# Gate and up of a SwiGLU kernel as two 128x64 weight halves side by side in the array

## The chip, the cores and the metric

The kernel runs on one core of a Trainium2 chip. The metric is the device time of one execution in microseconds; the time before is the median of three runs.

## The reference

```python
B, S, D, F = 1, 2048, 640, 1536          # all bfloat16
def reference(x, w_gate, w_up, w_down):
    g = jax.nn.silu(x @ w_gate)          # [S, D] @ [D, F]
    u = x @ w_up
    return (g * u) @ w_down              # [S, F] @ [F, D]
```

## The kernel before

The 2048 rows of x are worked through in four row blocks of 512 (`NSB`, `S_BLK`). All weights are kept in SBUF, with the contraction dimension D in five steps of 128 partitions (`KD`), and F in twelve chunks of 128 (`KF`). x is kept transposed in `xT`, so that a matmul takes a 128x128 piece of weights as its stationary operand and streams 512 columns of `xT`.

In a row block, for each chunk `fc` of F, `proj` (L202) makes five matmuls into a PSUM tile `pg` with the gate weights, then five into `pu` with the up weights; all ten are recorded at L204. Both tiles are of the tag "gu", which has four buffers of one bank each, so two chunks can be under way. `gate` (L217) lets ScalarE (ACT) take silu of `pg` into `sg` (L221) and VectorE (DVE) multiply `sg` with `pu` into the bf16 tile `aT` (L222). When the twelve chunks are done, the down product follows: twelve matmuls into `po_t` (L287) for the last 128 columns of the output, held transposed, and then for each of the four groups of 128 rows twelve matmuls into `po_a` (L316) for the first 512 columns. ScalarE copies these results out, and DMAs write them.

Row block 0 has a beginning of its own: `head` (L226) warms TensorE up with 20 matmuls (`pw`, L182), turns the first 256 rows of x by ten TensorE transposes (`pt`, L195), and does its first four chunks in pieces as the weights arrive (L250 and, through `proj`, L204). The last row block streams 508 rows instead of 512: the last four rows of x (`T`) get their gate and up on VectorE, by 96 multiply-and-sum instructions (`row_dots`, L153) that `do_dots` spreads out: two behind each of the first ten chunks of row blocks 1 to 3, and three at several places of the down products. The last 128 rows of the output are done in three column pieces of 256, 256 and 128.

The order of TensorE, ScalarE and GpSimd is fixed for the head by `keep_order` (L100), and that of VectorE and of the DMA queue of SyncE for the whole kernel; after the head TensorE's work follows the program in its own order: all gate and up chunks of a row block, po_t, po_a, and then the next row block. TensorE has a load of weights ahead of every matmul.

Of the kernel before, what the change touches and what calls it, by code (L numbers as in the profile page):

```python
# [10 lines left out]
def _body(  # L11
# [8 lines left out]
    nc = tc.nc  # L20
    P = nc.NUM_PARTITIONS
# [11 lines left out]
    KD = D // P  # L33
    KF = F // P
    S_BLK = 512
# [24 lines left out]
    xT = consts.tile([P, KD, S], bf16)  # L60
    wg_sb = consts.tile([P, KD, F], bf16)
    wu_sb = consts.tile([P, KD, F], bf16)
# [47 lines left out]
    def turn_x(c0, c1, k0=0, k1=KD):  # L110
        s_sl = slice(c0 * P, c1 * P)
        nc.sync.dma_start_transpose(out=xT[:, k0:k1, s_sl], in_=xt_v[s_sl, k0:k1])
# [22 lines left out]
    def turn_w(dst, src):  # L135
        for a in range(0, KF, WT_STEP):
            nc.sync.dma_start_transpose(
                out=dst[:, a : a + WT_STEP, :], in_=src[:, a : a + WT_STEP, :]
            )
# [24 lines left out]
    def row_tail():  # L164
        for _ in dots:
            pass
        nc.scalar.activation(row_s[:], row_g[:], ACT.Silu)
        nc.vector.tensor_tensor(
            out=aT[:, :, S - T : S], in0=row_s[:], in1=row_u[:], op=ALU.mult
        )  # L170
# [3 lines left out]
    def do_dots(n):  # L174
        for _ in range(n):
            next(dots, None)
# [25 lines left out]
    def proj(ps, w_sb, fc, sb, c0, c1, k0=0, k1=KD):  # L202
        for kd in range(k0, k1):
            nc.tensor.matmul(  # L204
                ps[:, c0:c1],
                lhsT=w_sb[:, kd, fc * P : (fc + 1) * P],
                rhs=xT[:, kd, sb * S_BLK + c0 : sb * S_BLK + c1],
                start=(kd == 0),
                stop=(kd == KD - 1),
            )  # L210

    def gu_tiles():
        pg = psum.tile([P, S_BLK], f32, tag="gu", name="pg", bufs=4)
        pu = psum.tile([P, S_BLK], f32, tag="gu", name="pu", bufs=4)
        return pg, pu

    def gate(pg, pu, sb, fc, n_s):  # L217

        s0 = sb * S_BLK
        sg = work.tile([P, S_BLK], f32, name="sg")  # L220
        nc.scalar.activation(sg[:, 0:n_s], pg[:, 0:n_s], ACT.Silu)  # L221
        nc.vector.tensor_tensor(  # L222
            out=aT[:, fc, s0 : s0 + n_s], in0=sg[:, 0:n_s], in1=pu[:, 0:n_s], op=ALU.mult
        )
# [46 lines left out]
    for sb in range(NSB):  # L271
        n_s = S_BLK if sb < NSB - 1 else S_BLK - T
        for fc in range(KF):
            if sb == 0 and fc < N_FIRST:
                continue
            pg, pu = gu_tiles()
            proj(pg, wg_sb, fc, sb, 0, n_s)
            proj(pu, wu_sb, fc, sb, 0, n_s)
            gate(pg, pu, sb, fc, n_s)
            if sb > 0 and fc < KF - 2:  # L280
                do_dots(2)


        n_t = (SUB if sb < NSB - 1 else SUB - 1) * P
        po_t = psum.tile([P, n_t], f32, tag="po_b", name="po_t")
        for kf in range(KF):
            nc.tensor.matmul(  # L287
                po_t[:],
                lhsT=wd_sb[:, kf, DA:D],
                rhs=aT[:, kf, sb * S_BLK : sb * S_BLK + n_t],  # L290
                start=(kf == 0),
                stop=(kf == KF - 1),
            )
        ot_t = outp.tile([P, n_t], bf16, name="ot_t")
        ot_q = outp.tile([P, n_t], bf16, name="ot_q")
        nc.scalar.copy(ot_t[:], po_t[:])  # L296
        do_dots(3)
        nc.vector.transpose(out=ot_q[:], in_=ot_t[:])  # L298
        for q in range(P // Q):
            nc.scalar.dma_start(  # L300
                out=out2[
                    sb * S_BLK : sb * S_BLK + n_t, DA + q * Q : DA + (q + 1) * Q
                ].rearrange("(i r) c -> r i c", r=Q),
                in_=ot_q[q * Q : (q + 1) * Q, :].rearrange("r (i c) -> r i c", c=Q),
            )

        for j in range(SUB):
            s0 = sb * S_BLK + j * P
            last = sb == NSB - 1 and j == SUB - 1
            cols = [(0, DA, "po_a")]  # L310
            if last:
                cols = [(0, DA // 2, "po_a"), (DA // 2, DA, "po_a"), (DA, D, "po_b")]
            for c0, c1, tag in cols:
                po = psum.tile([P, c1 - c0], f32, tag=tag, name="po_a")
                for kf in range(KF):
                    nc.tensor.matmul(  # L316
                        po[:],
                        lhsT=aT[:, kf, s0 : s0 + P],
                        rhs=wd_sb[:, kf, c0:c1],
                        start=(kf == 0),  # L320
                        stop=(kf == KF - 1),
                    )
                ot = outp.tile([P, c1 - c0], bf16, name="ot" if c1 < D else "ot_b")
                if c1 < D:
                    nc.scalar.copy(ot[:], po[:])  # L325
                    eng = nc.sync
                else:
                    nc.vector.tensor_copy(out=ot[:], in_=po[:])  # L328
                    eng = nc.sync
                if 0 < j and not last:  # L330
                    do_dots(3)
                if sb == NSB - 1 and j == ROW_J:
                    row_tail()
                eng.dma_start(out=out2[s0 : s0 + P, c0:c1], in_=ot[:])
        if sb == 0:
            turn_x(2 * SUB, 3 * SUB)
            turn_w(wuT, wut_v)
            turn_x(3 * SUB, 4 * SUB)
# [72 lines left out]
def kernel(tc, *args):  # L411
    _body(tc, *args)
    tc.close()
    tc.compile()
    _trim(tc.nc)
# [30 lines left out]
```

## Time and profile before

| | |
|---|---|
| median of 3 runs | 163.79 us (163.2, 163.79, 163.9) |
| profiled execution, its own time | 163.25 us |
| its span, first to last instruction | 161.9 us |
| TensorE matmuls (PE) busy | 159.6 us, 99% of the span, 818 instructions |
| TensorE weight loads (PEld) busy | 79.9 us, 49%, 818 instructions |
| VectorE (DVE) busy | 110.5 us, 68% |
| ScalarE (ACT) busy | 42.6 us, 26% |
| granted TensorE clock | 1.00 |

PE counts the time in which at least one matmul is under way; neighbouring matmuls overlap, so the sum of their durations is more than the busy time, and the distance of their starts is read from the chain of work that ended last, which strings together the groups in order of time. PEld counts weight loads, which can lie beside matmuls.

### The profile page before, as it was taken

The numbers are of one execution on the slowest core, as the hardware profiler recorded it, in microseconds if no ns is written. First come the engines' busy times: TensorE is split into PE (matmuls) and PEld (weight loads), VectorE is DVE, ScalarE is ACT, GpSimd is POOL, SyncE is SP. The second block draws the span as 40 slices with busy tenths as digits, with TensorE's granted clock in tenths as the row PEclk, the third lists the DMA queues.
The fourth block names the chain that finished last, engine by engine and source line by source line (L and its number), as shares of the span: only waits on it lengthen the run. The fifth ranks groups of instructions, "written<-read, shape, count | busy, mean of one in ns | idle before, by whom it ended". The sixth has DMA issues, their size and how long they took to land.

```text
span 161.9 us, 2159 instructions
## 1 busy us (share of the span) xinstructions
PE 159.6 (99%) x818; PEld 79.9 (49%) x818; DVE 110.5 (68%) x249; ACT 42.6 (26%) x74; POOL 0.6 (0%) x6
## 2 busy tenths in 40 slices
PE   9999999999999999999999999999999999999995
PEld 9885444444444444444444444444444444445454
DVE  1006223599469999989919999979964999993000
ACT  5032222112222222211222322221214222222121
POOL 1000000000000000000000000000000000000000
PEclk9999999999999999999999999999999999999999
DMA  7999999995089992003110000000310000000212
GB/s 228 280 345 348 363 209 241 230 190 100 32 186 139 241 225 58 0 0 34 65 65 4 0 0 2 0 0 4 64 66 32 0 0 0 0 4 0 52 37 73
DMA packets 41209, 15.86 MB, mean 98 GB/s; under 512 B 33264, under 2 KB 41072, under 8 KB 41200
## 3 DMA queue, kind: packets, MB, share of 16 engines
q1 hardware_dynamic: 32832, 14.81, 38.0%
q10 hardware_dynamic: 8368, 0.92, 3.7%
q8 instruction: 6, 0.10, 0.3%
q14 instruction: 3, 0.02, 0.1%
HBM read 6.88 MB, written 2.62 MB: 59 GB/s over the span
## 4 chain that ended last, share of the span: by engine, by line
PE 99%; DVE 0%; issue 0%
PE pu L204 32%; PE pg L204 31%; PE po_a L316 26%; PE po_t L287 6%; PE pg L250 2%; PE pw L182 1%; PE pt L195 1%; DVE ot_b L328 0%; DVE ones L108 0%
## 5 line engine op out<-in xcount | busy, mean ns | idle before, releaser
L204 PE MATMUL pu<-xT,wu_sb 128*128 128x512 bf16 (+2 forms) x260 | 59.3, 362 | 0.0
L204 PE MATMUL pg<-xT,wg_sb 128*128 128x512 bf16 (+2 forms) x240 | 56.9, 370 | 0.0
L222 DVE TENSOR_TENSOR aT<-sg,pu 128x512 bf16<-128x512 f32 (+1 forms) x48 | 32.5, 682 | 32.8 <-PE pu L204 32.8
L221 ACT ACTIVATE sg<-pg 128x512 f32<-128x512 f32 (+1 forms) x48 | 28.4, 597 | 71.1 <-PE pg L204 67.5
L316 PE MATMUL po_a<-wd_sb,aT 128*128 128x512 bf16 (+2 forms) x216 | 42.8, 358 | 0.0
L153 DVE SCALAR_TENSOR_TENSOR prod<-wgT,x_row 128x640 f32<-128x640 bf16 x48 | 39.4, 821 | 1.1
L153 DVE SCALAR_TENSOR_TENSOR prod<-wuT,x_row 128x640 f32<-128x640 bf16 x48 | 39.4, 822 | 1.0
L204 PEld LDWEIGHTS <-wu_sb 128*128 128x128 bf16 x260 | 25.4, 98 | 26.5 <-DMA wu_sb<-in_w_up_dram 0.2
L204 PEld LDWEIGHTS <-wg_sb 128*128 128x128 bf16 x240 | 23.5, 98 | 25.9
L316 PEld LDWEIGHTS <-aT 128*128 128x128 bf16 x216 | 20.7, 98 | 21.6
L325 ACT CAST ot<-po_a 128x512 bf16<-128x512 f32 (+1 forms) x17 | 9.5, 561 | 32.0 <-PE po_a L316 20.9
L287 PE MATMUL po_t<-aT,wd_sb 128*128 128x512 bf16 (+1 forms) x48 | 10.4, 366 | 0.0
L287 PEld LDWEIGHTS <-wd_sb 128*128 128x128 bf16 x48 | 4.7, 98 | 5.1
L328 DVE CAST ot_b<-po_a 128x128 bf16<-128x128 f32 x1 | 0.3, 292 | 9.9 <-PE po_a L316 9.9
L296 ACT CAST ot_t<-po_t 128x512 bf16<-128x512 f32 (+1 forms) x4 | 2.2, 559 | 11.6 <-PE po_t L287 11.6
L153 DVE DVE_READ_ACCUMULATOR prod<-wuT,x_row 128x1 f32 x48 | 4.0, 82 | 0.0
L153 DVE DVE_READ_ACCUMULATOR prod<-wgT,x_row 128x1 f32 x48 | 3.9, 82 | 0.0
L298 DVE STREAM_TRANSPOSE ot_q<-ot_t 128x512 bf16<-128x512 bf16 (+1 forms) x4 | 2.7, 678 | 1.7 <-ACT ot_t L296 1.7
L250 PE MATMUL pg<-xT,wg_sb 128*128 128x256 bf16 (+1 forms) x24 | 3.1, 307 | 0.0
L200 DVE COPY xT<-pt 128x384 bf16<-128x384 bf16 x2 | 0.7, 358 | 3.2 <-PE pt L195 3.2
L250 PEld LDWEIGHTS <-wg_sb 128*128 128x128 bf16 x24 | 2.6, 127 | 0.3
L182 PE MATMUL pw<-ones 128*128 128x128 bf16 x20 | 2.3, 313 | 0.3 <-DVE ones L108 0.3
(15 smaller groups left out, 8.0 us busy)
## 6 DMA issues: line engine op xcount, KB each, us to landing
wd_sb<-in_w_down_dram SPq DMA_DIRECT2D x1, 1920.0 KB, 14.6
out_dram<-ot SPq DMA_DIRECT2D x15, 128.0 KB, 1.7
wg_sb<-in_w_gate_dram SPq DMA_DIRECT2D x2, 640.0 KB, 6.7
wu_sb<-in_w_up_dram SPq DMA_DIRECT2D x2, 640.0 KB, 8.0
x_row<-in_x_dram SPq DMA_DIRECT2D x1, 640.0 KB, 4.9
wg_sb<-in_w_gate_dram SPq DMA_DIRECT2D x3, 128.0 KB, 3.5
wu_sb<-in_w_up_dram SPq DMA_DIRECT2D x1, 384.0 KB, 4.7
out_dram<-ot_q ACTq DMA_DIRECT2D x12, 32.0 KB, 2.1
```

What stands on the lines that cost most here:

```text
L153: nc.vector.scalar_tensor_tensor(out=prod[:], in0=wT[:, fc, :], scalar=1.0, in1=x_row[:, t, :], op0=ALU.mult, op1=ALU.mult, accum_out=acc[ ...
L182: nc.tensor.matmul(pw[:, 0:P], lhsT=ones[:].broadcast_to([P, P]), rhs=ones[:].broadcast_to([P, P]), start=True, stop=True,)
L195: nc.tensor.transpose(out=pt[:, kd - k0, :], in_=x_sb[:, c, kd * P : (kd + 1) * P], identity=ident[:],)
L204: nc.tensor.matmul(ps[:, c0:c1], lhsT=w_sb[:, kd, fc * P : (fc + 1) * P], rhs=xT[:, kd, sb * S_BLK + c0 : sb * S_BLK + c1], start=(kd == 0 ...
L221: nc.scalar.activation(sg[:, 0:n_s], pg[:, 0:n_s], ACT.Silu)
L222: nc.vector.tensor_tensor(out=aT[:, fc, s0 : s0 + n_s], in0=sg[:, 0:n_s], in1=pu[:, 0:n_s], op=ALU.mult)
L250: nc.tensor.matmul(pg[:, c0:c1], lhsT=wg_sb[:, kd, wslice(fc, fc + 1)], rhs=xT[:, kd, c0:c1], start=(kd == 0 and c0 == 0), stop=(kd == KD ...
L287: nc.tensor.matmul(po_t[:], lhsT=wd_sb[:, kf, DA:D], rhs=aT[:, kf, sb * S_BLK : sb * S_BLK + n_t], start=(kf == 0), stop=(kf == KF - 1),)
L296: nc.scalar.copy(ot_t[:], po_t[:])
L298: nc.vector.transpose(out=ot_q[:], in_=ot_t[:])
L316: nc.tensor.matmul(po[:], lhsT=aT[:, kf, s0 : s0 + P], rhs=wd_sb[:, kf, c0:c1], start=(kf == 0), stop=(kf == KF - 1),)
L325: nc.scalar.copy(ot[:], po[:])
```

## The change

In row blocks 1 to 3 a new helper, `proj_halves`, takes the place of `proj`. Each 128x128 piece of weights is split by its columns into two pieces of 128x64. The first is placed in the left half of the array (tile position 0, 0) and writes partitions 0 to 63 of the PSUM tile, the second in the right half (tile position 0, 64) and writes partitions 64 to 127. Both stream the same columns of `xT`, and both accumulate over the same five steps. Row block 0, the down product and all instructions of the other engines are as before. TensorE has 1178 matmuls and as many weight loads, where it had 818.

```diff
+    def proj_halves(ps, w_sb, fc, s0, n_s):
+        half = P // 2
+        for kd in range(KD):
+            for h in range(2):
+                f0 = fc * P + h * half
+                nc.tensor.matmul(
+                    ps[h * half : (h + 1) * half, 0:n_s],
+                    lhsT=w_sb[:, kd, f0 : f0 + half],
+                    rhs=xT[:, kd, s0 : s0 + n_s],
+                    start=(kd == 0),
+                    stop=(kd == KD - 1),
+                    tile_position=(0, h * half),
+                )
...
             pg, pu = gu_tiles()
-            proj(pg, wg_sb, fc, sb, 0, n_s)
-            proj(pu, wu_sb, fc, sb, 0, n_s)
+            if sb > 0:
+                proj_halves(pg, wg_sb, fc, sb * S_BLK, n_s)
+                proj_halves(pu, wu_sb, fc, sb * S_BLK, n_s)
+            else:
+                proj(pg, wg_sb, fc, sb, 0, n_s)
+                proj(pu, wu_sb, fc, sb, 0, n_s)
             gate(pg, pu, sb, fc, n_s)
```

## The prediction

> **What bounds the kernel now.** I read the page first: the span, the busy shares, the granted clock and the chain of work that ended last.
>
> ```profile
> span 161.9 us, 2159 instructions
> ...
> PE 159.6 (99%) x818; PEld 79.9 (49%) x818; DVE 110.5 (68%) x249; ACT 42.6 (26%) x74; POOL 0.6 (0%) x6
> ...
> PEclk9999999999999999999999999999999999999999
> ...
> PE 99%; DVE 0%; issue 0%
> PE pu L204 32%; PE pg L204 31%; PE po_a L316 26%; PE po_t L287 6%; PE pg L250 2%; PE pw L182 1%; PE pt L195 1%; DVE ot_b L328 0%; DVE ones L108 0%
> ```
>
> TensorE's matmuls are the whole chain, at a clock that never drops, and 63% of the chain is the gate and up products at L204, which the change rewrites. The view of waits has one row for TensorE over the whole execution:
>
> ```profile
> PE pw L182 <- DVE ones L108: 0.3, 1, 0.3
> ```
>
> After its start it waits for nobody. So the time is the sum of the matmuls' paces, and any nanosecond added between two matmuls is a nanosecond of the kernel. The paces stand in the chain in order of time (start us, us, what):
>
> ```profile
> 0.30 2.31 PE pw L182 x20
> ...
> 8.92 2.18 PE pg L204 x20
> ...
> 43.51 1.08 PE pg L204 x5
> 44.59 1.08 PE pu L204 x5
> ```
>
> A chain of five 512-column matmuls takes 1.08 us, 216 ns each; twenty of 256 columns take 2.18 us, 109 ns each. Twice 109 less 216 leaves 2 ns, a part of each matmul that does not depend on its columns; the rest is about 0.42 ns a column. Next the groups by shape, which give a single matmul's duration, and the page's groups for the weight loads (busy us, mean ns of one):
>
> ```profile
> L204 PE MATMUL pg<-xT,wg_sb 128*128 128x512 bf16 x160 | 39.8, 379 | 0.0
> ...
> L204 PE MATMUL pg<-xT,wg_sb 128*128 128x508 bf16 x60 | 14.8, 377 | 0.0
> ```
>
> ```profile
> L204 PEld LDWEIGHTS <-wu_sb 128*128 128x128 bf16 x260 | 25.4, 98 | 26.5 <-DMA wu_sb<-in_w_up_dram 0.2
> L204 PEld LDWEIGHTS <-wg_sb 128*128 128x128 bf16 x240 | 23.5, 98 | 25.9
> ```
>
> A matmul lasts 379 ns and the next starts after 216, so 163 ns of each are a tail that lies beside its successor. A load of 128x128 weights lasts 98 ns, and the timeline tells where it lies:
>
> ```profile
> 60.61 1.24 PE L204 MATMUL pg<-xT,wg_sb 128*128 128x512 bf16 x5
> ```
>
> ```profile
> 60.40 0.96 PEld L204 LDWEIGHTS <-wg_sb 128*128 128x128 bf16 x5
> ```
>
> The chain's first load starts at 60.40 and the matmul that uses it at 60.61, one pace later: each load runs under the matmul before it, and half of PEld's time is free.
>
> **The change, part by part.** The base is the profiled execution: span 161.9 us, its own time 163.25, so 1.35 us lie outside the span, and nothing in the change touches those. The median of the three runs is 163.79, 0.54 above, and the runs reach from 163.2 to 163.9. I add the sum to both and state the forecast on the median. A run differs from no change here by what exceeds 0.5%, 0.82 us.
>
> In row blocks 1 to 3 there are 3 x 12 chunks with 2 products of 5 steps: 360 matmuls with their loads become 720 and 720. Each new matmul fills one half of the array's columns and streams the same 512 (in block 3: 508) columns. The order on TensorE stays otherwise as it was: all the halves of a row block stand together, the two of a step next to each other, then the unchanged po_t and po_a. That makes six joints between the whole and the half form, one into and one out of each row block. Instructions of the other engines keep their number and order.
>
> *The second stream.* Halves that are in the array together cost one stream a step, as before: 0. Halves that stream one after the other cost one more pace: 240 x 216 + 120 x 214 ns = 77.5 us. The trace has no two matmuls streaming at once; the nearest row is that 163-ns tail, and a load besides: the array holds two matmuls and a load at the same time already. The two halves share neither weights nor array columns nor rows of the output, and nothing in the program orders one behind the other's end. I take 0, and 77.5 as the dearest rival. The Trainium skill, "TensorEngine Tiling (Array Packing)", section Key Properties, says that tiles load weights and multiply independently and in parallel; by it the term is 0 as well, and no row of before can show it.
>
> *The issue of 360 more pairs.* Each step has four instructions for TensorE in its 216 ns where it had two. The narrowest matmuls show how fast pairs can follow; these are the loads of the last 128-column tile, in the timeline:
>
> ```profile
> 159.08 0.66 PEld L316 LDWEIGHTS <-aT 128*128 128x128 bf16 x11
> ```
>
> (660 - 98) / 10 = 56 ns a pair. Two pairs need 112 of 216 ns, and 104 are spare: the streams hide it. The slow end is the warm-up above, 2.31 us for 20 pairs, 116 ns each: two would need 232, 16 ns more than a step, 360 x 16 ns = 5.8 us. The last tile runs behind matmuls at full pace, as the new pairs do, and the warm-up does not; I take 0 by the first, and on top the 2 ns that every matmul shows at every width, once for each added one: 360 x 2 ns = 0.7 us. If the halves hide that part under one another instead, it is -0.7.
>
> *The weight loads.* Two loads of 64 columns in place of one of 128. At the 98 ns that a whole one lasts, which a half one should not exceed, two in a row take 196 ns of a 216-ns step: hidden, with 20 ns to spare. In steady state the second half would simply run some tens of ns behind the first. If that cover is gone, a load that must wait for a matmul's end costs 56 ns (the pace above) to 98 ns a step: 20 to 35 us. I take 0. Here a page speaks against the change. The Trainium skill, "TensorE: Matmul & The Clock Gate", section The mechanism in Part 3, says that in a tiled array a weight load overlaps a running matmul only where their row groups differ. Both halves use all 128 rows, so by it no load would be hidden. The trace of before disagrees for the whole array: loads with the same rows lie under the matmul before them (60.40 against 60.61). For halves no row decides, and so it is the second rival.
>
> *The six joints.* The trace has none of this kind. The nearest is the change of weights and output from pu to po_t at full width; in the chain of row block 2:
>
> ```profile
> 107.18 1.08 PE pu L204 x5
> 108.26 1.94 PE po_t L287 x9
> ```
>
> 107.18 + 1.08 = 108.26: there is no gap. The least is therefore 0; the most is that the array empties and the next load stands bare, 163 + 98 = 261 ns, six times 1.6 us. I take the 163-ns tail alone, 1.0 us, since the load needs only its own half of the array. The same tiling page says that a switch of tiling mode drains TensorE; by it the term would be of this size too.
>
> *What is behind TensorE.* DVE is the closest engine. In row block 2 (columns: PE, PEld, DVE, ACT, POOL busy us):
>
> ```profile
> 84.40:110.00 25.60, 25.60 (x120) 11.58 (x119) 24.07 (x55) 6.81 (x12) 0.00 (x0) 1.00 0.00 1
> ```
>
> DVE is busy 24.07 of 25.60 us. It receives the same 24 tiles at the same pace or later; a slower TensorE gives it more room, and a gain of 0.7 us over three blocks leaves it below its limit. DMA stands at 0.00 there, so a third more instructions for the chip to fetch meet no traffic.
>
> The sum: 0 + 0.7 + 0 + 1.0 = +1.7 us. 163.25 + 1.7 = 165.0 against the profiled execution, and 163.79 + 1.7 = 165.5 on the median. By its own bounds the forecast's case runs from 163.79 to 163.79 + 0.7 + 1.6 = 166.1, and to 171.9 if pairs issue as slowly as in the warm-up.
>
> **The rivals.**
>
> *The halves take turns.* One stream of x enters the array at a time, and every step pays twice. For it: no row shows two streams, and all matmuls here start strictly one pace apart. Against it: the halves lie on different columns and outputs. 163.79 + 77.5 + 1.0 = 242.3 us (the added fixed part is in the added pace). Gate and up would then pace at 2.16 us for a chain.
>
> *The loads stand bare.* The halves stream together, but a half's load waits until a matmul has left its part of the array. For it: in the rows a load starts just when the matmul before it starts, so exactly one set of weights waits behind the running one, and it is open whether each half has such a place of its own. Against it: half of PEld's time is free, and two loads fit. A step grows by 56 to 98 ns, in all by 20 to 35 us: 163.79 + 1.7 + 20.2 = 185.7 to 200.8. A smaller part, from loads only partly bare or from slow issue, lies between 166 and 186.
>
> *Not slower.* The halves hide each other's fixed 2 ns, so a step takes 214 ns in place of 216, and the joints pass like the joint from pu to po_t, without a gap. Its place is each of the 360 steps; it decides if a joint costs under 0.12 us (0.7 / 6). For it: that joint without a gap. Against it: the fixed part is there at every width, also at 256 columns, where the next matmul has just as much to hide it. 163.79 - 0.7 = 163.1 us. That is within 0.5%; a larger gain would need something that no row hints at.
>
> **How the numbers follow.** The forecast's case has 0.49, the halves in turns 0.17, the bare loads (with partly bare ones and slow issue) 0.22, not slower 0.12. The range starts at the last rival's 163.1 and ends at the second's 200.8: it holds 0.49 + 0.22 + most of 0.12, about 0.82, and leaves out the turns. Slower by over 0.5% (above 164.6): the turns 0.17, the loads 0.22, and 0.44 of the forecast's case, as its sum of +1.7 passes 0.82 unless both small terms are under half of what I took: 0.83. Within 0.5%: the other 0.05 and 0.08 of the last rival, 0.13. Faster: 0.04, for a gain that the rows do not price.
>
> **What would show it.** In the profile after, the chain should show gate and up of row blocks 1 to 3 as groups of ten halves in about 1.08 to 1.1 us, the two matmuls of a step starting less than 100 ns apart, 1178 weight loads (818 + 360), and six gaps of 0.1 to 0.3 us at the joints. Starts 216 ns apart, groups of ten in 2.16 us, would show the turns. Chains of 1.36 to 1.57 us, with each load starting only at a matmul's end, would show bare loads. The forecast is wrong if the pace of a step leaves 214 to 222 ns, or if TensorE begins to wait for DVE or ACT.

## Result, and the profile after

The change takes 164.23 us (median of 14 runs, 163.83 to 164.65) where the kernel before takes 163.54 (14 runs, 163.03 to 163.94): +0.69 us, ratio 1.0039, interval 1.0027 to 1.0052. It is slower by less than half of the 1.7 us that were forecast. The profiled execution took 164.29 us with a span of 162.9, TensorE's clock at 1.00.

The page of the changed kernel has TensorE's groups as they were forecast in form:

```profile
PE 160.3 (98%) x1178; PEld 84.5 (52%) x1178; DVE 110.5 (68%) x249; ACT 42.7 (26%) x74; POOL 0.6 (0%) x6
...
L217 PE MATMUL pg<-xT,wg_sb 128*64 128x512 bf16 (+1 forms) x360 | 44.8, 379 | 0.0
...
L217 PEld LDWEIGHTS <-wg_sb 128*64 128x64 bf16 x360 | 20.1, 110 | 19.0 <-issue 1.3
L217 PEld LDWEIGHTS <-wu_sb 128*64 128x64 bf16 x360 | 20.4, 110 | 18.4
```

A half's matmul lasts 379 ns like a whole one, and its load of half as many weights 110 ns where a whole one lasts 98. The chain in order of time tells what they cost:

```profile
9.30 2.18 PE pg L204 x20
...
30.93 2.59 PE po_t L305 x12
33.52 10.36 PE po_a L334 x48
43.88 1.20 PE pg L217 x10
45.08 1.08 PE pu L217 x10
46.16 1.08 PE pg L217 x10
...
65.59 1.08 PE pg L217 x10
69.91 2.70 PE po_t L305 x12
...
82.96 1.20 PE pg L217 x10
...
108.98 2.69 PE po_t L305 x12
...
122.04 1.19 PE pg L217 x10
...
147.86 2.06 PE po_t L305 x12
149.91 11.07 PE po_a L334 x72
```

Ten halves take 1.08 us, to the last digit what five wholes took: the two halves of a step stream together, and the added pair costs nothing. Their loads lie beside each other too: 360 loads of 110 ns are 39.6 us, and PEld is busy with them for 20.1. Only two groups of a row block are longer. The first gate product takes 1.20 us instead of 1.08 (1.19 instead of 1.07 in the last block, where 508 columns are streamed). po_t behind the last up product takes 2.70 in place of 2.59 (2.06 against 1.95 in the last block). That is 3 x 0.12 + 3 x 0.11 = 0.69 us, at the six joints between the two forms, and nothing anywhere else.

The part of the chain behind the head can be compared without the head, whose end depends on when the first weights land. From the start of the twenty gate matmuls that follow the head's first up products to the end of the last po_a it is 149.91 + 11.07 - 9.30 = 151.68 us; in the profile before, whose first and last rows of this kind are

```profile
8.92 2.18 PE pg L204 x20
...
148.86 11.07 PE po_a L316 x72
```

it is 151.01. The difference is 0.67 us. I call this stretch the body below. Of the 1.0 us between the two profiled spans the other 0.38 is the head, 9.30 against 8.92.

How a joint looks is seen in the timeline around 43.8 us (start us, us, engine, line):

```profile
42.86 1.03 PE L334 MATMUL po_a<-wd_sb,aT 128*128 128x512 bf16 x4
43.29 0.10 PEld L334 LDWEIGHTS <-aT 128*128 128x128 bf16 x1
43.81 0.57 PEld L217 LDWEIGHTS <-wg_sb 128*64 128x64 bf16 x8 [0.42 <-issue]
43.81 0.84 PE L217 MATMUL pg<-xT,wg_sb 128*64 128x512 bf16 x6
```

The last whole matmul starts at 42.86 + 3 x 0.216 = 43.51. In the ordinary course the next load would start with it. Here it starts 0.30 us later, 0.09 past the point where the next matmul was due, and PEld is shown idle for 0.42 us on no semaphore ("issue"). The first halves start together with their loads. The other 0.02 to 0.03 us pass until the second step, which starts 0.24 us after the first and not 0.216.

### The profile page after: what moved, and what is told of

Its sections match the earlier page's. It is cut to its first block, busy times and chain, and to the rows that moved or that the text cites. A ratio compares the mean times of both kernels' runs of the same rounds, so it can differ in the third digit from the quotient of the medians.

```text
span 162.9 us, 2879 instructions
## 1 busy us (share of the span) xinstructions
PE 160.3 (98%) x1178; PEld 84.5 (52%) x1178; DVE 110.5 (68%) x249; ACT 42.7 (26%) x74; POOL 0.6 (0%) x6
## 4 chain that ended last, share of the span: by engine, by line
PE 95%; DMA 3%; SPq 1%; DVE 0%; issue 0%
PE po_a L334 26%; PE pg L217 24%; PE pu L217 24%; PE pu L204 8%; PE pg L204 7%; PE po_t L305 6%; DMA wu_sb<-in_w_up_dram 3%; SPq L118 1%; SPq L88 0%; DVE ot_b L346 0%
## 5 line engine op out<-in xcount | busy, mean ns | idle before, releaser
L217 PE MATMUL pg<-xT,wg_sb 128*64 128x512 bf16 (+1 forms) x360 | 44.8, 379 | 0.0
L217 PE MATMUL pu<-xT,wu_sb 128*64 128x512 bf16 (+1 forms) x360 | 44.7, 378 | 0.0
L217 PEld LDWEIGHTS <-wg_sb 128*64 128x64 bf16 x360 | 20.1, 110 | 19.0 <-issue 1.3
L217 PEld LDWEIGHTS <-wu_sb 128*64 128x64 bf16 x360 | 20.4, 110 | 18.4
L204 PE MATMUL pu<-xT,wu_sb 128*128 128x256 bf16 (+1 forms) x80 | 14.6, 326 | 0.1
L204 PE MATMUL pg<-xT,wg_sb 128*128 128x512 bf16 (+1 forms) x60 | 12.3, 344 | 0.0
L204 PEld LDWEIGHTS <-wu_sb 128*128 128x128 bf16 x80 | 7.7, 98 | 5.5 <-DMA wu_sb<-in_w_up_dram 0.3
L204 PEld LDWEIGHTS <-wg_sb 128*128 128x128 bf16 x60 | 5.9, 98 | 4.7
```

The costliest lines, as they stand in the source:

```text
L204: nc.tensor.matmul(ps[:, c0:c1], lhsT=w_sb[:, kd, fc * P : (fc + 1) * P], rhs=xT[:, kd, sb * S_BLK + c0 : sb * S_BLK + c1], start=(kd == 0 ...
L217: nc.tensor.matmul(ps[h * half : (h + 1) * half, 0:n_s], lhsT=w_sb[:, kd, f0 : f0 + half], rhs=xT[:, kd, s0 : s0 + n_s], start=(kd == 0), ...
```

## Experiments

The theory is that of the joints: a change of the form of the weights costs about 0.11 us of TensorE's time, and split steps cost nothing. Its rival is that of the pairs: 0.69 us over 360 added pairs is 1.9 ns each, which is what the prediction had put down as a fixed part of every matmul.

**All of it in halves.** po_t and po_a are split in the same way, row block 0 is included, and only the head and the last 128 rows stay whole.

```diff
-            if sb > 0:
...
-            else:
-                proj(pg, wg_sb, fc, sb, 0, n_s)
-                proj(pu, wu_sb, fc, sb, 0, n_s)
+            proj_halves(pg, wg_sb, fc, sb * S_BLK, n_s)
+            proj_halves(pu, wu_sb, fc, sb * S_BLK, n_s)
...
+            for h in range(2):
+                nc.tensor.matmul(
+                    po_t[h * 64 : (h + 1) * 64, :],
+                    lhsT=wd_sb[:, kf, DA + h * 64 : DA + (h + 1) * 64],
...
+                    tile_position=(0, h * 64),
+                )
...
+                    if last:
...
+                    else:
+                        for h in range(2):
+                            nc.tensor.matmul(
+                                po[h * 64 : (h + 1) * 64, :],
+                                lhsT=aT[:, kf, s0 + h * 64 : s0 + (h + 1) * 64],
...
+                                tile_position=(0, h * 64),
+                            )
```

> Everything behind the head is done in halves: gate and up of all row blocks, po_t, and po_a but for the last 128 rows. 668 steps are split where the change split 360, but only two joints are left, one behind the head and one before the last 128 rows. Joint theory (a joint costs 0.11 us, an added pair nothing): +0.23 us over the kernel before, ratio 1.001, less than the change's +0.69. Pair theory (0.69 us / 360 = 1.9 ns for each added pair, joints free): +1.3 us, ratio 1.008.

Measured: 163.83 us against 163.38, ratio 1.003 (1.0018 to 1.0041), +0.45 us. That lies between the two, nearer to the joints. Its body decides it:

```profile
9.45 2.18 PE pg L204 x20
...
157.28 3.41 PE po_a L333 x36
```

157.28 + 3.41 - 9.45 = 151.24, 0.23 above the body before: two joints, and nothing for 308 more split steps than the change has.

**One product in halves.** Only the first gate product of each of the three row blocks is split.

```diff
-            if sb > 0:
+            if sb > 0 and fc == 0:
                 proj_halves(pg, wg_sb, fc, sb * S_BLK, n_s)
-                proj_halves(pu, wu_sb, fc, sb * S_BLK, n_s)
             else:
                 proj(pg, wg_sb, fc, sb, 0, n_s)
-                proj(pu, wu_sb, fc, sb, 0, n_s)
+            proj(pu, wu_sb, fc, sb, 0, n_s)
```

> Only the gate product of the first chunk of each of the row blocks 1 to 3 is in halves: 15 split steps, and six joints as in the change. Joint theory: +0.69 us, the whole of what the change costs, ratio 1.004. Pair theory: 15 x 1.9 ns = +0.03 us, ratio 1.000.

Measured: 164.35 us against 163.38, ratio 1.0061 (1.0045 to 1.0076), +0.97 us. Fifteen split steps cost at least as much as 360, so the pairs are out. The body is 151.69 us, 0.68 above that of before, as with the change itself:

```profile
9.05 2.18 PE pg L204 x20
...
149.72 11.02 PE po_a L333 x71
```

**Gate in halves, up in wholes.** 72 joints.

```diff
                 proj_halves(pg, wg_sb, fc, sb * S_BLK, n_s)
-                proj_halves(pu, wu_sb, fc, sb * S_BLK, n_s)
+                proj(pu, wu_sb, fc, sb, 0, n_s)
```

> Gate in halves, up in wholes, in all chunks of row blocks 1 to 3: 180 split steps and 72 joints. Joint theory: 36 x (0.118 + 0.110) = +8.2 us, about 171.8 us. Pair theory: 180 x 1.9 ns = +0.3 us. If a joint's price lies in what else happens at the change of stage (new tiles, new reader) and not in the form of the weights, the joints between gate and up are free, and it is about +0.35 us for the three from po_a.

Measured: 171.69 us, ratio 1.0501 (1.0482 to 1.0521), +8.31. In the chain every product is longer by its joint, 1.20 and 1.19 for 1.08, also where nothing but the form of the weights changes between gate and up of one chunk:

```profile
49.78 1.19 PE pu L204 x5
50.97 1.20 PE pg L217 x10
52.17 1.19 PE pu L204 x5
53.35 1.20 PE pg L217 x10
```

The rows of the body are these:

```profile
9.23 2.18 PE pg L204 x20
...
157.40 11.02 PE po_a L334 x71
```

8.31 / 72 is 0.115 us a joint; by the body, 157.40 + 11.02 - 9.23 = 159.19 us, it is 8.18 / 72 = 0.114. The price is that of the form, not of the stage.

**Left half first, then right half.** The two loops of the helper are swapped.

```diff
-        for kd in range(KD):
-            for h in range(2):
+        for h in range(2):
+            for kd in range(KD):
```

> The change with the loops swapped: all five steps of the left half, then all five of the right half, in each product. If matmuls start in program order and two are in the array at once only where neighbours in that order lie in different halves, the five steps of a half follow at 216 ns and only the fifth of one half and the first of the next lie together: 8 paces in place of 5 for a product, 1.73 us, 72 x 3 x 0.216 = +46.6 us over the change, about 210.8 us. If a half's matmuls may overtake the other half's, it stays at the change's 164.2 us. If the two halves never stream together in this order, 10 paces, +77.7 us, about 242 us.

Measured: 164.80 us, ratio 1.0087 (1.0072 to 1.0103), +1.42. I had expected +46.6 over the change if matmuls start in program order, and nothing if the halves may overtake each other; it is some 0.6 to 0.7. The timeline of TensorE shows why:

```profile
43.37 0.38 PE L334 MATMUL po_a<-wd_sb,aT 128*128 128x512 bf16 x1
43.68 1.30 PE L217 MATMUL pg<-xT,wg_sb 128*64 128x512 bf16 x9
44.78 0.38 PE L217 MATMUL pu<-xT,wu_sb 128*64 128x512 bf16 x1
44.81 0.38 PE L217 MATMUL pg<-xT,wg_sb 128*64 128x512 bf16 x1
45.00 1.06 PE L217 MATMUL pu<-xT,wu_sb 128*64 128x512 bf16 x8
```

The first up matmul starts at 44.78, before the tenth gate matmul at 44.81, which stands ahead of it in the program. The halves do not follow one common order: each goes through its own matmuls at its own pace. The right half runs about one step behind the left for the whole row block, and at its end one pace is left over. The body, 150.56 + 11.02 - 9.16 = 152.42 by the rows below, is 1.41 above that of before: 0.68 for the joints and 0.73, about 3 x 0.22 us and a little, for that step in each of the three blocks.

```profile
9.16 2.18 PE pg L204 x20
...
150.56 11.02 PE po_a L334 x71
```

**The kernel before, measured as a changed one.**

> The kernel before, unchanged, measured as a changed one: what the comparison calls a difference where there is none. If joints are all that the earlier kernels add, +0.45 us with two joints (0.23 expected) and +0.97 with six (0.69 expected) leave 0.2 to 0.3 us each that must be chance of the runs or of the head's transfers: a ratio that strays from 1 by up to 0.0015, and a head that starts up's first matmul anywhere between 6.6 and 7.1 us. If the difference belongs to the changed kernels, this one comes out at 1.000 with its head at 6.6 us, as in the profile of before.

Measured: 163.62 us against 163.28, ratio 1.0016 (1.0005 to 1.0027). The same program came out 0.34 us late by the medians, 0.26 by the ratio, and the interval leaves out 1; its body is 148.96 + 11.02 - 8.98 = 151.00, that of before to 0.01. So the medians of a single series stray by some 0.3 us without any change of the program, and the bodies do not.

```profile
8.98 2.18 PE pg L204 x20
...
148.96 11.02 PE po_a L316 x71
```

**Quarters.** `proj_halves` gets a number of parts: 4 for all of row block 1, and 2 for gate with 4 for up in row block 2; row block 3 is whole.

```diff
-    def proj_halves(ps, w_sb, fc, s0, n_s):
-        half = P // 2
+    def proj_halves(ps, w_sb, fc, s0, n_s, parts=2):
+        half = P // parts
...
-            for h in range(2):
+            for h in range(parts):
```

> Row block 1 in quarters (four 128x32 pieces of weights to a step, eight instructions for TensorE in a pace), row block 2 with gate in halves and up in quarters, row block 3 in wholes. If every part of the array takes its weights and its stream by itself, a step stays at 216 ns, a product at 1.08 us; a joint between halves and quarters costs about 0.11 us if it is the change of the form that empties the array, and nothing if only the way between whole and split does. With 1 + 1 joints in row block 1 and 25 in row block 2: 27 x 0.114 = +3.1 us, about 166.5; without the price between halves and quarters +0.5 us. If eight instructions do not fit into 216 ns at the 28 ns each that 56 ns a pair bound, a product in quarters takes longer than 1.08 us.

Measured in a single execution: 166.7 us, where 166.5 was expected of 27 joints that all cost 0.114. Its body is 152.36 + 11.02 - 9.23 = 154.15, 3.14 more than before's, 0.116 a joint.

```profile
9.23 2.18 PE pg L204 x20
...
152.36 11.02 PE po_a L337 x71
```

In the timeline at the entry into row block 1, twelve quarters, three steps of four, take 0.83 us, as six halves took 0.84 after the change. The next product, twenty quarters, takes 1.08 us: eight instructions fit into a pace.

```profile
43.74 0.55 PEld L217 LDWEIGHTS <-wg_sb 128*32 128x32 bf16 x16 [0.42 <-issue]
43.74 0.83 PE L217 MATMUL pg<-xT,wg_sb 128*32 128x512 bf16 x12
```

```profile
45.01 1.08 PE pu L217 x20
```

In row block 2 the way from halves to quarters and back costs as much as that from wholes:

```profile
84.08 1.19 PE pu L217 x20
85.28 1.20 PE pg L217 x10
86.47 1.19 PE pu L217 x20
```

**Streams of 128 columns.** A helper goes through the 512 columns in four pieces, with whole weights in row block 1 and halves in row block 2.

```diff
+    def proj_narrow(ps, w_sb, fc, s0, cols):
+        for c in range(4):
+            for kd in range(KD):
+                for h in range(P // cols):
+                    f0 = fc * P + h * cols
+                    nc.tensor.matmul(ps[h * cols : (h + 1) * cols, c * P : (c + 1) * P],
+                        lhsT=w_sb[:, kd, f0 : f0 + cols],
+                        rhs=xT[:, kd, s0 + c * P : s0 + (c + 1) * P], ...,
+                        tile_position=(0, h * cols))
```

> Row blocks 1 and 2 stream 128 columns at a time, four to a product, row block 1 with whole weights, row block 2 with halves; row block 3 whole with 508. It measures the cover that the prediction gave the weight loads. Whole: 56 ns each as in the last tile of before, 20 to a product, 1.12 us. Halves: also 1.12 us if two 64-column loads fit under a 128-column stream, in all about +2.2 us (24 x 2 x 0.04 and two joints). If the loads of halves have less room, and follow each other at the 110 ns that one lasts, 2.2 us a product and +27 us.

Measured in a single execution: 165.29 us, +2.0. In the chain, in the order of the two row blocks, twenty wholes and forty halves:

```profile
46.88 1.12 PE pu L231 x20
```

```profile
83.28 1.24 PE pg L231 x40
84.52 1.12 PE pu L231 x40
85.63 1.12 PE pg L231 x40
```

Both take 1.12 us, 56 ns a step. The loads of the halves in the groups by shape:

```profile
L231 PEld LDWEIGHTS <-wu_sb 128*64 128x64 bf16 x480 | 14.1, 110 | 0.0
```

Two loads that last 110 ns each hide under a stream that is a quarter of the change's, with four instructions in 56 ns. The joint is there too (1.24).

**Once more, three on one chip.** The kernel before, the change and the all-halves kernel, without an edit.

> The kernel before once more, beside the next two on the same chip: 1.000 within 0.001 if the 0.26 us by which it strayed in the run before were chance; again about 1.0015 if whatever is measured as the changed kernel comes out late.

> The change as it is, to be set against the other two of this call and not against the runs of before. Joint theory: 0.68 us over the kernel before as measured in the same way, six joints of 0.114. Pair theory gives the same here, and differs in the next.

> 668 split steps and two joints, against the other two of this call. Joint theory: 0.45 us below the change and 0.23 above the kernel before. Pair theory: 0.6 us above the change.

Measured against one set of 25 runs of before (163.39 us):

| | median | ratio | interval | profiled execution, us | head ends, us | body, us |
|---|---|---|---|---|---|---|
| before | 163.44 | 1.0005 | 0.9990 to 1.0020 | 163.48 | 9.16 | 151.00 |
| the change, six joints | 163.93 | 1.0039 | 1.0026 to 1.0053 | 163.63 | 8.64 | 151.68 |
| all halves, two joints | 163.61 | 1.0013 | 0.9999 to 1.0028 | 163.27 | 8.71 | 151.23 |

The heads and bodies come from the same pair of rows of each chain. The change lies 0.49 us over the kernel before here, where 0.68 was expected, and the all-halves kernel, with almost twice the split steps, lies 0.32 below the change, where 0.45 was expected. The bodies, at 0.68 and 0.23 above before, are as the joints have them to 0.01 us. The table also shows where the times stray: the change took 164.29 us with a head that ends at 9.30 in the profile above, and 163.63 with one that ends at 8.64 here, and its body is the same. In all twelve profiled executions, what is left of the time beside head and body is 3.30 to 3.33 us.

The experiments point to no version that beats both kernels: a split step is as fast as a whole one and never faster, so without joints a split kernel is at best level with the kernel before.

## Why the prediction was wrong

It had the direction and the mechanism, the streams beside each other and the price at the joints, and the result lies in its range, which is wide (163.1 to 200.8). Its sum, +1.7 us against +0.69, was more than twice too large, and so the chance for slower by over 0.5% (0.83) was far too high: the change lies within 0.5%, at 0.4%. Of the 1.0 us too much, 0.7 are the added pairs and 0.3 the joints. The chance also rested on a slip: the sum was said to pass 0.82 us unless both small terms were under half their size, but with the pairs at 0 any joints under 0.82 us in all are enough, and that is what came.

- **The second stream, 0.** Right: ten halves in 1.08 us. The halves in turns (242.3 us) are out.
- **The issue of 360 more pairs, +0.7. This is the step that failed.** The 2 ns that each matmul shows beside its columns were charged once for each added matmul, as if TensorE paid them in one row. The runs show them once for each step, whatever its parts: a step stays at 216 ns with two and with four matmuls (1.08 us a product), and 308 more split steps add nothing to the body. Neither the +0.7 nor the lower bound of -0.7, at which the halves hide that part altogether, came; the term is 0. The cover of 104 ns that it claimed for the issue was there and larger: four instructions fit into 56 ns.
- **The weight loads, 0.** Right in size, but not for the reason given. A half's load lasts 110 ns and not at most 98, so two in a row would take 220 ns, more than the step of 216. They run beside each other (20.1 us busy for 39.6 us of loads), and cost nothing even under a 128-column stream. The bare loads (185.7 to 200.8 us) are out. The rule of the Trainium skill that stood for them ("TensorE: Matmul & The Clock Gate", section The mechanism in Part 3) does not hold for halves: both use the same rows, and ten of them take 1.08 us. The measurement decides.
- **The six joints, +1.0.** The mechanism was right, the size was not: 0.114 us each, 0.68 together. The prediction took the whole tail of 163 ns as lost. What is lost is 0.09 us before the next load starts and some 0.03 until the second step on the way in, 0.11 us on the way out. The Trainium skill says that a change of tiling mode drains TensorE ("TensorEngine Tiling (Array Packing)", section Key Properties). The trace agrees in that every change costs a gap, also between halves and quarters (1.19 and 1.20 for 1.08). A whole drain is not shown: by the records, whose ends are modelled, the last whole matmul ends at 42.86 + 1.03 = 43.89 us, and the first halves start at 43.81.
- **What is behind TensorE, 0.** Right: DVE is busy for 110.5 us as before, and the chain behind the head has no piece of it but the last copy (ot_b).
- **Not slower (163.1 us).** Its condition, a joint under 0.12 us, is met (0.114), but the gain that was to pay for the joints is missing: the step stays at 216 and not 214 ns. Its -0.7 for the added pairs is as far from the measured 0 as the forecast's +0.7.

## What to carry to other kernels

On a kernel that TensorE's paces fill, count the joints between forms of weights and not the split steps: the form may be changed twice a stage, but not between gate and up of each chunk, where it cost 8.3 us. Splitting full 128x128 weights gains nothing, since both halves stream all the columns; it is nearly free, which could matter where a piece of work fills only half or a quarter of the array and another can be put beside it (no run here tries that). And where a difference of 0.2 us decides, compare the stretch of the chain that the change can touch: it repeated to 0.01 us where two medians of one program, of 11 and 15 runs, differed by 0.34.

## What was not expected of the hardware

- The halves of the array take their matmuls independently: with all of the left half ahead of the right in the program, they still ran together, a matmul of the next product started before one of the product ahead of it (44.78 against 44.81 us), and the cost was one step in each row block, not the 46.6 us that program order would cost.
- Two loads of 64 columns, 110 ns each in the records, are hidden under 56 ns a step.
- A change between wholes and halves, wholes and quarters, or halves and quarters costs 0.11 to 0.12 us.
